# Four tiles of the first expert taken from six attention blocks and multiplied beside the routing, with the next weights split at other places

## The chip, the cores and the metric

One core of one Trainium2 chip runs the whole program. The metric is the device time of one execution in microseconds (us). In the profile PE is TensorE (matmuls) and PEld its weight loads, DVE is VectorE, ACT is ScalarE, POOL is GpSimd and SP is SyncE, which only starts transfers. A line number such as L853 is a line of the kernel before.

## What is computed

Three layers follow each other: an attention over pooled keys, a mixture of experts in which each token goes to one expert, and a mixture in which each token goes through all experts.

```python
# B, H, S, D = 4, 8, 576, 64; pool = 8
k_p = k.reshape(B, H, Sp, pool, D).mean(axis=3)
v_p = v.reshape(B, H, Sp, pool, D).mean(axis=3)
attn = softmax(scale * np.matmul(q, k_p.transpose(0, 1, 3, 2)))
x = (attn @ v_p).transpose(0, 2, 1, 3).reshape(B * S, H * D)
...
# first mixture: N, D, E, F = 2304, 512, 8, 1024
logits = x @ w_gate
e_idx = np.argmax(logits, axis=1)
for e in range(E):
    mask = e_idx == e
    h = np.maximum(x[mask] @ w1[e], 0.0)
    out[mask] = gate_w[mask, None] * eom[mask, e, None] * (h @ w2[e])
...
# second mixture: P from 8 alternating normalisations of exp(logits)
for e in range(E):
    h = np.maximum(x @ w1[e], 0.0)
    out += P[:, e:e + 1] * (h @ w2[e])
```

With the inputs that are used, expert 0 gets 1217 of the 2304 tokens, which is ten tiles of 128 positions; four other experts have 5, 2, 3 and 2 tiles.

## The kernel before, in words

**The planned part.** The attention, the routing of the first mixture and the first expert's first tile are not emitted as they are written. `Notes`, a subclass of `Plan`, records each operation with what it reads and writes, with a cost and with a number; `Plan.run` is a list scheduler that gives each engine, whenever it is free in the model, the ready operation with the lowest number plus `late`. A larger `late` puts an operation behind others, and `after` makes all operations recorded from then on wait for one earlier operation. What comes out is a fixed order for each engine. All these instructions carry the line of the recorder, L1293. Accumulation groups of matmuls stay together unless `whole` is false. The four PSUM tiles of this part are called ab.

**The attention** works on nine blocks of 256 rows in the order 0, 1, 2, 3, 4, 5, 8, 6, 7. `weigh` multiplies the probabilities with the values and divides; `write_rows` writes the block's rows of x to `rowd` in DRAM; `top1` turns the gate logits of a range of the 18 token tiles into one-hot rows `oh` (called at blocks 3, 8, 6 and 7). `between` loads the first expert's weights in eight pieces into the six raw buffers `wr` and splits each into a high and a low 16-bit part, which later stand in `w1` and `w2` (slots wa and wb).

**The routing.** `route` ranks all tokens by expert: it counts the one-hot rows with matmuls (`ones`, `prior`, `tri`), makes a one-hot row per token tile on VectorE, and by 18 more matmuls gets `idx`, the list of tokens in order of expert. 18 indirect transfers (`gather`, on POOL's queue) bring 128 rows each from `rowd` into one of eight buffers `raw` (`GB` = 8). `columns` transposes a gathered tile with four matmuls against the identity and splits it into high and low parts of `xT` (ScalarE copies the high part, VectorE subtracts). `stages` and `registers` put the tile counts and the starts of the experts into registers.

**A tile of an expert** is `one`: 96 matmuls of 128x128 for the first product (three 16-bit products for each of 4 x 8 blocks, L853), the ReLU on ScalarE (L858), the cast to 16 bit and the subtraction that gives the low part, both on VectorE (L859, L860), 24 matmuls of 128x512 for the second product (L868), the scaling and adding into `x2` (L873) and the row maximum (L876), on VectorE.

**The first expert.** Ten sets of columns and tile 0 stand in the planned part. Then `moe1` runs a loop over c = 1 to 8, each under a branch on the tile count, with four more sets of columns behind c = 1 and c = 2 and one piece of the next expert's weights behind each (`w[1].step(c - 1)`: a scaled copy on ScalarE and a subtraction on VectorE, L785). Tile 9 follows under its own branch.

**Then** `ahead` gives POOL the preparation of the second mixture's first weights (L976 to L1013: loads, sums, casts and stores, all on POOL), and nested branches (`stage`, `item`) go through the other experts. In the first two tiles of an expert the eight pieces of the next expert's weights are split: `pieces` says which stand ahead of the first product, between its two halves and behind both.

Of the kernel before, what the change touches and what calls it, by code (L numbers as in the profile page):

```python
# [10 lines left out]
F32 = mybir.dt.float32  # L11
# [372 lines left out]
LATE = {"scores": -50, "weigh": 150, "key_layout": 100}  # L384


def attention(g):
# [12 lines left out]
    def load(b, i):  # L400
        kv[b, i] = put(load_kv, b, i)
# [4 lines left out]

    load(0, 0)
# [17 lines left out]
    for at, n in enumerate(order):  # L425
        qT = g.tile([P, 2, H, P], F16, "qT", 2)
        put(q_transpose, qb[n], qT)
        if at + 3 < NB:
            qb[order[at + 3]] = put(q_load, order[at + 3])
        ex = g.tile([P, 2, H, SP], F32, "ex", 2)  # L430
        for hf in range(2):
            put(scores, n, qT, ex, hf)
        eT = g.tile([P, 2, 2, CH, P], F16, "eT", 2)
        for tail in (False, True):
            put(exp_transpose, ex, eT, tail)
        xs = g.tile([P, 2, H, VC - 1], F32, "xs", 3)
# [233 lines left out]
def stages(g):  # L670
# [46 lines left out]
    nc.vector.tensor_copy(g.stgi, stg[:, 0:3])  # L717
# [12 lines left out]
def registers(g):  # L730
# [6 lines left out]
        min_val=0, max_val=NT,  # L737
    )
# [8 lines left out]
class Weights:  # L747
# [19 lines left out]
    def raw(self, i):  # L767
        return self.g.wr[(8 * self.stage + i) % RAW]
# [26 lines left out]
GB = 8  # L795


def gather(g, j):

    gr = g.gat[:, j % GB]  # L800
    g.nc.gpsimd.indirect_dma_start(
        out=gr,
        out_offset=None,
        in_=g.rowd,
        in_offset=bass.IndirectOffsetOnAxis(ap=g.idx[:, j:j + 1], axis=0),
        bounds_check=N - 1,
        oob_is_err=False,
    )
    g.rows[j] = gr


def gathered(g, first, last):
    for j in range(first, last):
        columns(g, j, g.rows.pop(j))
        if j + GB < NT:
            gather(g, j + GB)


def columns(g, j, gr):
# [8 lines left out]
    hi, lo = [g.xT[:, s, :, j * P:(j + 1) * P] for s in range(2)]  # L828
# [4 lines left out]
def one(g, w, xt, j, cm, middle=None):  # L833
# [14 lines left out]
    for m, ph in enumerate(phs):  # L848
# [10 lines left out]
        nc.vector.tensor_copy(hs[:, 0, sl], hr[:, sl])  # L859
# [21 lines left out]
def moe1(g, first):  # L881
# [9 lines left out]
    xts = []  # L891
    for i in range(4):
        xt = g.xt.tile([P, 2, KC, P], F16, name=f"xt{i}")
        xts.append(xt)
# [9 lines left out]
    def item(r, c, xt):  # L904
# [1226 lines left out]
def attention_moe_moe(ctx: ExitStack, tc, q, k, v, wg, wo, w1, w2, wgb, w1b, w2b, out):  # L2131
# [50 lines left out]
    g.stgi = g.per.tile([P, 3, E], I32, name="stgi")  # L2182
# [31 lines left out]
    first = Weights(g, 0, w1[0], w2[0])  # L2214

# [14 lines left out]
    with ExitStack() as c:  # L2230
# [3 lines left out]
        attention(g)  # L2234
        g.tile = Arena(wb).tile
        route(g)
        g.notes.late = 300
        for i in range(6):
            g.nc.scalar.activation(
                g.x2[:, i * 3:i * 3 + 3, :].rearrange("p t c -> p (t c)"),  # L2240
                g.zero.to_broadcast([P, 3 * DM]), AF.Copy,
            )
# [81 lines left out]
```

## Time and profile before

| what | value |
|---|---|
| median of 3 runs | 1787.71 us (1787.49 to 1789.68) |
| the profiled execution | 1778.33 us, its span 1776.6 us |
| PE busy | 1693.8 us (95%) |
| PEld busy | 1475.0 us (83%) |
| DVE busy | 1267.4 us (71%) |
| ACT busy | 1023.1 us (58%) |
| POOL busy | 280.8 us (16%) |

Times in the trace count from the start of the span. The attention's last matmul ends at 117.42, the loop over the first expert's tiles begins at 153.23 and its tile 9 at 242.28, the second expert begins at 256.65 and the second mixture's work near 411. In a row of the timeline the first number is the start, the second the duration of the group, "x24" the number of instructions in it, and the bracket the idle time of the engine ahead of it with what ended it. In the table by stretch each engine's busy time stands with its number of instructions; PEclk is TensorE's granted clock as a share of the full 2.4 GHz.

### The profile page before, as it was taken

The page shows a single profiled execution, that of the slowest core. Times are in us where ns is not written, and L with a number is a line of the kernel's source. Part 1 is how long each engine was busy: PE and PEld are TensorE (multiplying, and loading weights), DVE is VectorE, ACT ScalarE, POOL GpSimd, SP SyncE. Part 2 cuts the span into 40 slices and gives each one's busy share as a digit, 9 for nine tenths or more (in the row PEclk, how much of TensorE's full clock was granted, in tenths as well). Part 3 has the DMA queues.
Part 4 walks back from the last instruction along what each step waited for, and adds up shares of the span by engine and source line. Part 5 has one row for each costly group of instructions (what it writes and reads, how often), then busy time and mean ns, then how long its engine had stood idle before and what let it go on. Part 6 is the DMA issues. An engine that isn't in the chain of part 4 may idle for free. (4 is left out here: it accounts for less than half of the span.)

```text
span 1776.6 us, 40042 instructions
## 1 busy us (share of the span) xinstructions
PE 1693.8 (95%) x17079; PEld 1475.0 (83%) x17079; DVE 1267.4 (71%) x2262; ACT 1023.1 (58%) x1872; POOL 280.8 (16%) x300
## 2 busy tenths in 40 slices
PE   5769998897999999999999999999999999999997
PEld 4657765666998899889888988898899889888986
DVE  7885567667896885787588567856876786587664
ACT  4743221435577775776577557756765775576542
POOL 7833778200000000000000000000000000000011
PEclk9989999998999999999999999999999999999999
DMA  9625434447331242243133313422441242234211
GB/s 301 164 72 179 138 120 160 136 158 301 103 134 56 88 141 37 48 109 107 27 82 114 78 25 81 137 47 37 114 125 25 60 133 71 37 72 125 102 54 42
DMA packets 83167, 183.83 MB, mean 103 GB/s; under 512 B 27664, under 2 KB 35856, under 8 KB 81168
## 3 DMA queue, kind: packets, MB, share of 16 engines
q1 hardware_dynamic: 68912, 131.66, 22.3%
q0 software_dynamic: 14048, 49.29, 13.0%
q8 instruction: 145, 2.38, 0.5%
q14 instruction: 62, 0.51, 0.1%
HBM read 121.16 MB, written 59.77 MB: 102 GB/s over the span
## 5 line engine op out<-in xcount | busy, mean ns | idle before, releaser
L1797 PEld LDWEIGHTS <-w1c 128*128 128x128 f16 x6720 | 604.0, 98 | 64.2 <-issue 2.2
L1896 PEld LDWEIGHTS <-hs 128*128 128x128 f16 x6048 | 590.6, 98 | 69.8 <-issue 1.9
L1797 PE MATMUL ua<-xc,w1c 128*128 128x256 f16 (+1 forms) x3840 | 426.7, 262 | 0.8 <-DVE xc L1460 0.6
L1896 PE MATMUL da<-x,hs 128*128 128x256 f16 x2592 | 318.2, 273 | 1.4 <-ACT z L1434 0.9
L1959 POOL DMA_DIRECT2D sums<-x x54 | 45.9, 850 | 1252.0 <-ACT x L1436 1217.0
L1797 PE MATMUL uc<-xc,w1c 128*128 128x256 f16 (+1 forms) x1920 | 213.1, 262 | 0.7 <-DVE xc L1460 0.5
L1817 DVE TENSOR_TENSOR u<-u,uc 128x512 f32<-128x512 f32 x144 | 99.0, 687 | 75.9 <-ACT u L1434 61.0
L1817 DVE TENSOR_TENSOR p<-p,ub 128x512 f32<-128x512 f32 x72 | 49.5, 687 | 140.8 <-PE ub L1797 140.8
L1434 ACT COPY u<-ua 128x512 f32<-128x512 f32 x144 | 83.9, 583 | 86.8 <-PE ua L1797 85.3
L1460 DVE TENSOR_TENSOR hs<-h,hs 128x512 f16<-128x512 f32 x144 | 99.2, 689 | 43.2 <-ACT hs L1434 43.2
L1460 DVE TENSOR_TENSOR hs<-u,hs 128x512 f16<-128x512 f32 x144 | 99.2, 689 | 39.2 <-ACT hs L1434 39.2
L1436 ACT ACTIVATE u<-u 128x512 f32<-128x512 f32 x144 | 91.0, 632 | 38.6 <-DVE u L1817 38.6
L858 ACT ACTIVATE wa<-ph 128x512 f32<-128x512 f32 x42 | 25.1, 597 | 150.7 <-PE ph L853 78.7
L1797 PE MATMUL ub<-xc,w1c 128*128 128x256 f16 (+1 forms) x960 | 106.3, 262 | 0.0
L1896 PE MATMUL da<-w2r,hs 128*128 128x256 f16 x864 | 106.1, 273 | 0.0
L1896 PE MATMUL db<-x,hs 128*128 128x256 f16 x864 | 106.1, 273 | 0.0
L1896 PE MATMUL dc<-x,hs 128*128 128x256 f16 x864 | 106.1, 273 | 0.0
L1896 PE MATMUL dc<-w2r,hs 128*128 128x256 f16 x864 | 106.1, 273 | 0.0
L868 PEld LDWEIGHTS <-wa 128*128 128x128 f16 x504 | 46.8, 98 | 70.4 <-DVE wa L860 13.0
L1434 ACT CAST hs<-p 128x512 f16<-128x512 f32 x144 | 89.3, 620 | 26.4 <-DVE p L1460 26.1
L1460 DVE TENSOR_TENSOR hs<-p,hs 128x512 f16<-128x512 f32 x144 | 99.0, 687 | 0.6 <-ACT hs L1434 0.6
L1436 ACT ACTIVATE p<-p 128x512 f32<-128x512 f32 x72 | 45.2, 628 | 86.2 <-DVE p L1817 86.2
(271 smaller groups left out, 2592.3 us busy)
## 6 DMA issues: line engine op xcount, KB each, us to landing
raw<-in_moe_w_dram SPq DMA_DIRECT2D x56, 512.0 KB, 4.0
wr<-in_moe_w_dram SPq DMA_DIRECT2D x54, 512.0 KB, 4.2
sums<-x POOLq DMA_DIRECT2D x54, 512.0 KB, 5.1
xc<-cspill SPq DMA_DIRECT2D x14, 1792.0 KB, 7.3
cspill<-xc SPq DMA_DIRECT2D x8, 896.0 KB, 4.5
sums<-x SPq DMA_DIRECT2D x9, 512.0 KB, 3.4
x<-sums SPq DMA_DIRECT2D x9, 512.0 KB, 3.6
wa<-in_k_dram SPq DMA_DIRECT2D x4, 1024.0 KB, 10.7
```

Source lines behind the costliest of these rows:

```text
L858: nc.scalar.activation(hr[:, sl], ph, AF.Relu, scale=HSC)
L868: nc.tensor.matmul(py, hs[:, a, k, :], w.w2[:, b, k, :], start=(k == 0 and t == 0), stop=(k == FC - 1 and t == 2),)
L1434: self.nc.scalar.copy(o, x)
L1436: self.nc.scalar.activation(o, x, func, scale=scale)
L1460: lambda: e.tensor_tensor(o, x, y, op=op), reads, writes, late,
L1797: nc.tensor.matmul(o, g.w1c[:, l, a, k, f * P:(f + 1) * P], g.xc[:, pr, r, b, k, :], start=(first and fi == 0 and n == 0), stop=(n == 5), ...
L1817: lambda: nc_.tensor_tensor(o_[0], o_[0], x_[0], op=ALU.add),
L1896: nc.tensor.matmul(t[x][0][:, lo], g.hs[:, sl[f // 2], l, a, f % 2, :], g.w2c[r][:, b, f, :], start=(first and n == 0), stop=(n == 11), sk ...
L1959: lambda: nc.gpsimd.dma_start(sums, x, accum_op=ALU.add), xk, [sk],
```

## The change

- `early_rows` ranks the tokens of blocks 0 to 5 (twelve token tiles) that belong to expert 0, for the first four tiles of 128: a count, a rank, twelve one-hot rows with twelve matmuls, and an index of four columns. `top1` is called after block 5 for tiles 8 to 11 in addition. Four indirect transfers bring the rows into two of the raw weight buffers (wr2 and wr3), and four calls of `columns` make xt0 to xt3 of them.
- `early_tiles` multiplies these four tiles in the planned part, with `late` 300 and not ahead of the last block's transposes of probabilities. ScalarE keeps the unscaled results in the gather buffers; `early_out` scales them after the routing.
- `full` says which of the four early tiles had 128 tokens. A tile that had fewer is multiplied again in a branch behind the loop; five registers (`s_a`) carry this.
- The routing's gathers go in the order 4, 5, ..., 17, 0, ..., 3. The planned part ends with tile 4, and the loop runs over c = 5 to 8 with two weight pieces behind each.
- The other experts' weight pieces move: none ahead of the first product, one (piece 0 or 5) between the halves, four or two behind both. The cast to 16 bit in `one` goes from VectorE to ScalarE. The raw buffers of later stages are shifted by two.
- Two transfers write zeros to rows of `rowd` that a gather of tiles 0 to 11 can touch before they are written; `x2` is cleared in seven pieces, for tiles 4 to 17.

**VectorE at the end of the attention.** x holds a block's results, ab the PSUM tiles, wa the row sums. Before:

```order
L1293 SCALAR_TENSOR_TENSOR x_97<-ab_277,x_97 128x2x512
L1293 TENSOR_REDUCE lgt<-x_97 128x32
L1293 SCALAR_TENSOR_TENSOR x_97<-ab_275,x_97 64x2x128
L1293 TENSOR_REDUCE mx<-lgt 128x6
L1293 TENSOR_TENSOR eq<-lgt,mx 128x48
L1293 TENSOR_TENSOR eq<-eq,rev 128x48
L1293 TENSOR_REDUCE fi<-eq 128x6
L1293 TENSOR_SCALAR wa<-ab_276 128x8
```

After, with the last early one-hot rows (out of iof), the early index (xT out of ab_296) and the early columns xt:

```order
L1446 TENSOR_SCALAR x_97<-iof_117,xT 128x128 x2
L1446 SCALAR_TENSOR_TENSOR x_97<-ab_294,x_97 128x2x512
L1446 TENSOR_SCALAR xT<-ab_296 128x4
L1446 TENSOR_SCALAR wa<-ab_295 128x8
L1446 TENSOR_TENSOR xT<-xT,ab_296 128x4
L1446 RECIPROCAL wa<-wa 128x8
L1446 TENSOR_TENSOR x_97<-ab_295,wa 128x640
L1446 SCALAR_TENSOR_TENSOR x_97<-ab_293,x_97 64x2x128
L1446 TENSOR_TENSOR xt_171<-ab_293,xt_171 128x512
```

The index is complete at its fifth row, the first subtraction of a gathered tile is the ninth, and the last blocks' divisions and logits stand behind it.

**TensorE behind the attention's last matmul.** oh holds the one-hot rows of all tokens, wa the first expert's weights. Before:

```order
L1293 MATMUL ab_274<-xT,x_97 128x81
L1293 LDWEIGHTS oh
L1293 MATMUL ab_277<-ones_115,oh 128x128
L1293 MATMUL ab_277<-ones_115,oh 16x128
L1293 LDWEIGHTS wb
L1293 MATMUL ab_275<-prior,wb 128x144
```

After:

```order
L1446 MATMUL ab_296<-xT,x_97 128x81
L1446 LDWEIGHTS wa
L1446 MATMUL ab_294<-xt_171,wa 128x128
L1446 LDWEIGHTS oh
L1446 MATMUL ab_293<-ones_115,oh 128x128
L1446 MATMUL ab_293<-ones_115,oh 16x128
L1446 MATMUL ab_295<-wa 128x512
L1446 LDWEIGHTS wb
L1446 MATMUL ab_296<-prior,wb 128x144
```

84 matmuls of the first early tile stand ahead of the routing's first, and its other 12 and one of its second product ahead of the ranking with prior. The early tiles' other matmuls stand between the later steps of the routing.

```diff
@@ attention
-        if n in (3, 8, 6, 7):
-            put(top1, *{3: (0, 8), 8: (16, 18), 6: (8, 14), 7: (14, 16)}[n])
+        if n in (3, 5, 8, 6, 7):
+            put(top1, *{3: (0, 8), 5: (8, 12), 8: (16, 18), 6: (12, 14), 7: (14, 16)}[n])
+        if n == 5:
+            put(early_rows)
@@ Weights
     def raw(self, i):
-        return self.g.wr[(8 * self.stage + i) % RAW]
+        return self.g.wr[(8 * self.stage + 2 * (self.stage > 0) + i) % RAW]
@@
+NE = 4
+EB = 6
+ORDER = [*range(NE, NT), *range(NE)]
...
+def early_rows(g):
...
+    for t in range(T):
+        ohp = new([P, P], BF16, "eohp", 3)
+        nc.vector.tensor_scalar(
+            ohp, g.iof16, lof[:, 0, t:t + 1], 1.0, op0=ALU.is_equal, op1=ALU.mult
+        )
+        nc.tensor.matmul(
+            px[:, 0, 0:2 * NE], ohp, ohv[:, t].rearrange("p x j -> p (x j)"),
+            start=(t == 0), stop=(t == T - 1),
+        )
...
+    for c in range(NE):
+        gather_rows(g, g.early[c], idx[:, c:c + 1], EB // 2 * S - 64)
+    for c in range(NE):
+        columns(g, g.early[c], g.xts[c])
+
+
+def early_tiles(g, w):
+
+    for c in range(NE):
+        product(g, w, g.xts[c], lambda py, c=c: g.nc.scalar.copy(g.early[c], py), c)
...
+def early_out(g):
...
+    nc.vector.tensor_tensor(ce, g.cm[:, 0, 0:NE], g.full, op=ALU.mult)
+    for c in range(NE):
+        nc.vector.tensor_scalar(g.x2[:, c], g.early[c], ce[:, c:c + 1], None, op0=ALU.mult)
...
+def product(g, w, xt, out, half):
+
+    nc = g.nc
+    hr, hs = g.hid[0]
...
@@ one
-        nc.vector.tensor_copy(hs[:, 0, sl], hr[:, sl])
+        nc.scalar.copy(hs[:, 0, sl], hr[:, sl])
@@ moe1
-            pieces = (((0,), (1, 2), (3, 4)), ((5,), (6,), (7,)))[c]
+            pieces = (((), (0,), (1, 2, 3, 4)), ((), (5,), (6, 7)))[c]
...
-    for c in range(1, 9):
+    for c in range(NE + 1, 9):
         first_tiles(c)
-        if c < 3:
-            gathered(g, NT - GB * (3 - c) // 2, NT - GB * (2 - c) // 2)
-        w[1].step(c - 1)
+        i = c - NE - 1
+        if i < 2:
+            gathered(g, NT - GB * (2 - i) // 2, NT - GB * (1 - i) // 2)
+        w[1].step(2 * i, 2 * i + 1)
+    with tc.If(g.s_a[NE] > 0):
+        for c in range(NE):
+            with tc.If(g.s_a[c] > 0):
+                one(
...
@@ the planned part
         attention(g)
+        g.notes.late, g.notes.after = 300, g.spread
+        early_tiles(g, first)
+        g.notes.late, g.notes.after = 0, None
...
+        early_out(g)
         gathered(g, 0, NT - GB)
-        one(g, first, g.xT[:, :, :, 0:P], slice(0, 1), g.cm[:, 0, 0:1])
+        one(
+            g, first, g.xT[:, :, :, NE * P:(NE + 1) * P], slice(NE, NE + 1),
+            g.cm[:, 0, NE:NE + 1],
+        )
```

## Rows read from the trace of the kernel before

**Rows 1.** The busy time of each engine by stretch, for two stretches.

```profile
core 0: us, PE busy (x) PEld busy (x) DVE busy (x) ACT busy (x) POOL busy (x), PEclk, DMA share, GB/s
80.00:116.00 36.00, 31.09 (x624) 26.92 (x624) 34.49 (x77) 20.23 (x25) 13.55 (x8) 0.97 0.33 75
117.40:153.20 35.80, 22.21 (x204) 16.36 (x203) 26.87 (x113) 11.61 (x17) 22.40 (x22) 0.76 0.48 152
```

**Rows 2.** TensorE's timeline from the attention's last matmul to the loop's last tile.

```profile
113.03 4.39 PE L1293 MATMUL ab<-xT,x 128*128 128x81 f16 x70 [1.02 <-DVE x L1293]
120.42 0.38 PE L1293 MATMUL ab<-ones,oh 128*128 128x128 bf16 x2 [3.00 <-DVE oh L1293]
...
126.27 2.09 PE L1293 MATMUL ab<-wb 128*128 128x36 bf16 x18 [3.97 <-POOL wb L1293]
...
136.29 2.35 PE L1293 MATMUL ab<-xT,wa 128*128 128x128 f16 x24
...
153.23 5.52 PE L853 MATMUL ph<-xT,wa 128*128 128x128 f16 x96 [0.94 <-DVE x L1293]
158.59 5.34 PE L868 MATMUL py<-wa 128*128 128x512 f16 x24
163.77 1.91 PE L827 MATMUL py<-ident,raw 128*128 128x128 f32 x16
165.52 5.52 PE L853 MATMUL ph<-xT,wa 128*128 128x128 f16 x96
...
242.28 5.52 PE L853 MATMUL ph<-xT,wa 128*128 128x128 f16 x96
```

**Rows 3.** Timelines of VectorE, POOL and TensorE, from the index to the first gathered tile.

```profile
128.61 0.17 DVE L1293 TENSOR_TENSOR idx<-wb,ab 128x18 int32<-128x18 f32 x1
129.08 1.27 POOL L1293 DMA_INDIRECT raw<-rowd,idx  x1 [1.72 <-DVE wb L1293]
130.66 1.00 POOL L1293 DMA_INDIRECT raw<-rowd,idx  x1 [0.31 <-issue]
132.72 1.12 PE L1293 MATMUL ab<-ident,raw 128*128 128x128 f32 x4 [4.36 <-DMA raw<-rowd,idx]
134.54 0.69 DVE L1293 TENSOR_TENSOR xT<-ab,xT 128x512 f16<-128x512 f32 x1 [2.91 <-ACT xT L1293]
```

**Rows 4.** VectorE's timeline: a wait near the attention's end, and the routing's one-hot rows.

```profile
117.45 0.17 DVE L1293 TENSOR_SCALAR wa<-ab 128x8 f32<-128x8 f32 x1 [1.43 <-PE ab L1293]
...
124.23 3.86 DVE L1293 TENSOR_SCALAR wb<-iof,wb 128x128 bf16<-128x128 bf16 x16
```

**Rows 5.** Timelines of TensorE and VectorE: experts two and three, weight splits L785.

```profile
256.65 7.15 PE L853 MATMUL ph<-xt,wb 128*128 128x128 f16 x96 [2.86 <-DVE xt L897]
270.48 3.78 DVE L785 SCALAR_TENSOR_TENSOR wa<-wr,wa 128x1024 f16<-128x1024 f32 x2
274.33 5.66 PE L853 MATMUL ph<-xt,wb 128*128 128x128 f16 x96
288.31 5.52 PE L853 MATMUL ph<-xt,wb 128*128 128x128 f16 x96
328.77 2.35 DVE L785 SCALAR_TENSOR_TENSOR wb<-wr,wb 128x1024 f16<-128x1024 f32 x2
334.42 5.52 PE L853 MATMUL ph<-xt,wa 128*128 128x128 f16 x96
```

**Rows 6.** TensorE's timeline at the starts of experts three and five.

```profile
323.38 5.52 PE L853 MATMUL ph<-xt,wa 128*128 128x128 f16 x96 [2.02 <-PEq L925]
...
380.41 5.52 PE L853 MATMUL ph<-xt,wa 128*128 128x128 f16 x96 [1.15 <-PEq L925]
391.98 5.52 PE L853 MATMUL ph<-xt,wa 128*128 128x128 f16 x96
```

**Rows 7.** POOL's timeline: first load and last store of the second mixture's weights.

```profile
178.27 0.58 POOL L976 DMA_DIRECT2D raw<-in_moe_w_dram  x1 [24.59 <-PE py L827]
...
323.81 0.68 POOL L1006 DMA_DIRECT2D w2spill<-raw  x1 [0.30 <-POOL raw L1002]
```

More of the change, by code (lines that the diff above doesn't have):

```diff
@@ L405, in sums @@
         vp[b] = put(pool_sum, nc.gpsimd if b else nc.vector, kv[b, 1])
+    none = g.tile([64, DM], F32, "none")
+    nc.gpsimd.memset(none, 0.0)
+    for b in range(EB // 2 - 1):
+        nc.sync.dma_start(g.rowd[b * S + 512:(b + 1) * S, :], none)
     load(0, 0)
@@ L435, in attention @@
             put(exp_transpose, ex, eT, tail)
+        g.spread = len(g.notes.tasks) - 1
         xs = g.tile([P, 2, H, VC - 1], F32, "xs", 3)
@@ L737, in registers @@
         min_val=0, max_val=NT,
+    )
+    _, g.s_a = nc.values_load_multi_w_load_instructions(
+        tab[:, 3 * E:3 * E + NE + 1], engines=[ET.PE, ET.DVE, ET.Activation, ET.SP],
+        min_val=0, max_val=NE,
     )
@@ L795, with gather_rows @@
 GB = 8
-def gather(g, j):
-    gr = g.gat[:, j % GB]
+NE = 4
+EB = 6
+ORDER = [*range(NE, NT), *range(NE)]
+def gather_rows(g, gr, idx, n=N):
     g.nc.gpsimd.indirect_dma_start(
@@ L803, in gather @@
         out_offset=None,
-        in_=g.rowd,
-        in_offset=bass.IndirectOffsetOnAxis(ap=g.idx[:, j:j + 1], axis=0),
-        bounds_check=N - 1,
+        in_=g.rowd[0:n, :],
+        in_offset=bass.IndirectOffsetOnAxis(ap=idx, axis=0),
+        bounds_check=n - 1,
         oob_is_err=False,
     )
+def gather(g, i):
+    gr = g.gat[:, i % GB]
+    j = ORDER[i]
+    gather_rows(g, gr, g.idx[:, j:j + 1])
     g.rows[j] = gr
 def gathered(g, first, last):
[L813 to L816, printed above, removed]
@@ new lines, in product @@
+def product(g, w, xt, out, half):
+    nc = g.nc
+    hr, hs = g.hid[0]
+    any2 = bank2(g)
+    for m in range(2):
+        ph = any2[:, m].rearrange("p (f n) -> p f n", n=P)
+        for mm in range(4):
+            f = 4 * m + mm
+            for k in range(KC):
+                for t, (a, b) in enumerate(PASSES):
+                    nc.tensor.matmul(
+                        ph[:, mm, :], w.w1[:, a, k, f * P:(f + 1) * P], xt[:, b, k, :],
+                        start=(k == 0 and t == 0), stop=(k == KC - 1 and t == 2),
+                    )
+        sl = slice(4 * m, 4 * m + 4)
+        nc.scalar.activation(hr[:, sl], ph, AF.Relu, scale=HSC)
+        nc.scalar.copy(hs[:, 0, sl], hr[:, sl])
+        nc.vector.tensor_tensor(hs[:, 1, sl], hr[:, sl], hs[:, 0, sl], op=ALU.subtract)
+    py = bank2(g)[:, 0]
+    g.notes.whole = False
+    for k in range(FC):
+        for t, (a, b) in enumerate(PASSES):
+            nc.tensor.matmul(
+                py, hs[:, a, k, :], w.w2[:, b, k, :],
+                start=(k == 0 and t == 0), stop=(k == FC - 1 and t == 2),
+            )
+    g.notes.whole = True
+    out(py)
@@ L820, in columns @@
+def columns(g, gr, xt):
     nc = g.nc
@@ L827, in columns @@
         nc.tensor.transpose(pt[:, k, :], gr[:, k * P:(k + 1) * P], g.ident)
-    hi, lo = [g.xT[:, s, :, j * P:(j + 1) * P] for s in range(2)]
+    hi, lo = [xt[:, s] for s in range(2)]
     nc.scalar.copy(hi, pt)
@@ L890, in moe1 @@
     ]
[L891 to L894, printed above, removed]
+    xts = g.xts
     def fetch(c, j):
@@ L2181, in attention_moe_moe @@
     g.cm = g.per.tile([P, E, NT], F32, name="cm")
-    g.stgi = g.per.tile([P, 3, E], I32, name="stgi")
+    g.stgi = g.per.tile([P, 4, E], I32, name="stgi")
     g.idx = g.keep.tile([P, NT], I32, name="idx")
@@ L2214, in attention_moe_moe @@
     first = Weights(g, 0, w1[0], w2[0])
+    g.early = [g.wr[2 + i // 2][:, i % 2 * DM:(i % 2 + 1) * DM] for i in range(NE)]
+    g.xts = []
+    for i in range(4):
+        t = g.xt.tile([P, 2, KC, P], F16, name=f"xt{i}")
+        g.xts.append(t)
+    g.full = g.per.tile([P, NE], F32, name="full")
     def between(n):
@@ L2237, in attention_moe_moe @@
         g.notes.late = 300
-        for i in range(6):
+        for i in range(NE, NT, 2):
             g.nc.scalar.activation(
-                g.x2[:, i * 3:i * 3 + 3, :].rearrange("p t c -> p (t c)"),
-                g.zero.to_broadcast([P, 3 * DM]), AF.Copy,
+                g.x2[:, i:i + 2, :].rearrange("p t c -> p (t c)"),
+                g.zero.to_broadcast([P, 2 * DM]), AF.Copy,
             )
```

75 lines of the change are left out of this document (72 added, 3 removed).

## The prediction

> **What bounds the kernel now.** I read the busy time by stretch first, then VectorE's rows and waits in the attention, then the chain from the token list to the first gathered tile, then TensorE's rows up to the second layer. The chain that ended last holds only the final output writes, so the bound of each stretch is read from the engines. The reader should see three things.
>
> First, late in the attention VectorE is full: 34.49 us of the 36 between 80 and 116 us [rows 1]. Work added there before the last block's logits moves the end of the attention by its own length.
>
> Second, from the last attention matmul (113.03 + 4.39 = 117.42) to the first tile of the expert loop (153.23) TensorE works 22.2 of 35.8 us at a mean granted clock of 0.76 [rows 1, 2]. It waits 3.00 for the last one-hot and 4.36 for the first gathered rows, and what follows that wait runs slowly: 24 matmuls in 2.35 us, 98 ns each, against 5.36 / 96 = 56 ns in the loop [rows 2, 3]. This is the room that the change wants to fill.
>
> Third, in the loop TensorE hardly waits. A tile is 5.36 for the first product (153.23 to 158.59) and 5.18 for the second (to 163.77): 10.54 us, and 1.75 more if four tiles are transposed behind it [rows 2]. The eight tiles of the loop take 89.05 (153.23 to 242.28). The second layer starts behind the last expert, so what moves that point moves the end.
>
> The profiled execution took 1778.33 (span 1776.6), 9.4 less than the median of the runs, 1787.71. The sum below is a difference and is put on the median.
>
> **The change part by part.**
>
> *a. The early ranking, inside the attention: +11, from +6 to +15.* Before the last one-hot VectorE gets 35 more instructions: twelve one-hot rows of 128x128 at 3.86 / 16 = 0.24 [rows 4], 2.9; four subtractions of 128x512 at 0.69 [rows 3], 2.7; 19 small ones at up to 0.17 each, as the index's own [rows 3], 3.2 at most. Between other instructions small ones overlap, so I take 8.0 for 8.8. With VectorE full, all of it shows.
>
> Then comes a wait that the attention did not have. From the index's write (128.78) to the first transpose of gathered rows (132.72) the kernel takes 3.94, and VectorE's subtraction starts at 134.54, 5.8 after the index [rows 3]; at full clock 0.5 less, 5.2. In the new order only three VectorE instructions (1.3 us) lie between the early index and the first early subtraction, so VectorE stands still for 3.9. TensorE stands before the first early transposes too, with 63 matmuls of block 8 behind it that the next VectorE instruction needs; that adds 1.4. Back come the 1.43 wait near the end [rows 4], where TensorE will be ahead, and 0.5 of smaller waits. 8.0 + 5.3 - 1.9 = 11.4, rounded to 11. Low end: no gather wait. High end: TensorE falls to its 1.2 GHz level behind that wait, as the matmuls at 136.29 ran, and the 63 matmuls take twice their 4.0 (4.39 / 70 each [rows 2]).
>
> The four early gathers cost POOL 1.3 each (1.00 + 0.31) [rows 3], 5.2 us where it has nothing else: taken as nothing. The two transfers of zeros (0.26 MB) stand in SP's queue behind six weight loads and ahead of the next keys: nothing, at worst 0.26 MB at the 75 GB/s of the late attention [rows 1], 3.5. Block 8's row writes now wait on SP for the early gathers; the writes of blocks 6 and 7 queue behind them, but are made later anyway.
>
> *b. From the last attention matmul to the loop: 35.8 becomes 67.5, +31.7.* TensorE has to do five tiles at 10.54 (52.7), ten sets of transposes at 1.91 / 4 = 0.48 [rows 2] (4.8) and the routing's own matmuls (2.9, an estimate from its first and its largest group, 0.38 and 2.09 [rows 2], some of it at full clock): 60.4 us, all at full clock since it hardly pauses. By the new order it still waits: after the last routing matmul 36 matmuls (2.0) stand ahead of the first gathered rows that are 4 us off, so 2.0; gathers come every 1.3 us and four sets of transposes (0.48 each) follow each other without filler, 2.1; the hidden tile's one buffer is handed over twice at the end, 1.5; 0.6 elsewhere. 6.2 in all, and 0.9 to enter the loop, as now [rows 2]. ScalarE and VectorE get six short steps per tile, of 0.7 or less, beside it. The routing itself starts 0.5 to 1 later because the first early product stands ahead of its first matmul; that lies inside the 60.4.
>
> *c. The loop: -42.9.* Eight tiles become four. The two with transposes stay (12.29 each, 153.23 to 165.52 [rows 2]); the other six take 64.5, 10.75 each, and two of them stay: 89.05 - 24.6 - 21.5 = 42.9. Each now carries two weight splits, 2.35 us of VectorE [rows 5] in 10.5.
>
> *d. The skipped repeat: +1.5.* The block that would multiply early tiles again is jumped over by all engines. Its nearest rows are the jumps at the end of an expert: 1.15 and 2.02 of TensorE [rows 6]; all of it shows, since TensorE has nothing queued. Bounds: 0.9, the present entry of the loop [rows 2], and 2.9, the longest wait at an expert's start [rows 5]. The five more registers are read in that entry: nothing.
>
> *e. The other experts: -4, from -8 to +6.* Expert two's first two tiles take 17.68 and 13.98 (256.65 to 288.31) instead of 10.54: 10.6 lost, because eight weight splits stand between VectorE's own steps of the tile, at 1.89 each while POOL prepares the second layer's weights, against 1.18 when POOL is done (3.78 and 2.35 a pair) [rows 5]. Expert three's first takes 11.04, with POOL's work over [rows 5 to 7]. Now one split stands between the halves and four behind both, and the cast to 16 bit leaves VectorE for ScalarE. With POOL idle I count no stall. With POOL busy the four splits (7.6) and the tile's other steps outlast the 10.5 of TensorE and the next tile waits some 3. But POOL's work, 145 us long (178.27 to 323.81) [rows 7], starts 25 us into the loop, so 42 us later than now, and then lies beside experts three and four as well. Three contended experts at 3, with 1.6 of slow clock once (7.15 against 5.52 [rows 5]), are 10.6. Today's losses are 10.6 in expert two, 0.5 in three and 1.0 each in the split tiles of four and five (391.98 - 380.41 = 11.57 [rows 6]), 13.1; the cast gives 1 more: -3.5, rounded to -4.
>
> The row shows a split slowed by 60% beside POOL. The Trainium skill (SBUF — State Buffer, section "SBUF: two separate sides") says more: VectorE with two SBUF inputs and GpSimd share a port that one of them holds for its whole instruction while the other is blocked. By that rule every split behind a POOL step would lose up to the whole step, experts three and four would pay about what expert two paid, and the sum would end above zero; by the row it stays below. The rows agree with a loss, not with a full block each time.
>
> **Sum:** 11 + 31.7 - 42.9 + 1.5 - 4 = -2.7, so 1785.0. The 42 us taken out of the loop are nearly all put back ahead of it, because the room there held only 35.8 - 22.2 = 13.6 idle us and some 6 of slow clock, and the ranking costs 11.
>
> **The rivals.**
>
> *The early work finds room (1777).* If VectorE's queue has been ordered so that the early gathers land while it is still busy, a is 6 instead of 11, and with gathers ahead of TensorE b loses 3 of its 6.2: -2.7 - 5 - 3 = -10.7. For it: POOL and SP are idle there. Against it: VectorE's 34.49 of 36, and three instructions between index and subtraction.
>
> *POOL's work meets the later splits (1795).* Slower: the splits of experts three and four run beside POOL's preparation. Stage e becomes +6 if each pays some 5 us, half of what expert two paid: -2.7 + 10 = +7.3. It decides from the point where their splits take over 1.6 us instead of 1.18. For it: the 42 us shift. Against it: the cast is gone from VectorE and the four splits stand behind both halves.
>
> *The change does not do what it says (1827).* If the first expert had fewer than 512 tokens in blocks 0 to 5, tiles would be multiplied again, up to 42.2 more: -2.7 + 42.2 = +39.5. Evaluating the reference's routing on its own inputs gives 571, and a first expert of ten tiles, which the loop's nine plus one show; hardly possible.
>
> **How the numbers follow.** 0.2% is 3.6 us, about what a measurement tells from no change. Forecast 0.50, its own range 1780 to 1791; room found 0.20; POOL's work 0.28; repeat 0.02. The forecast lies below -3.6 in about 0.42 of its cases and above +3.6 in 0.05, the second case wholly below, the third nearly wholly above: faster 0.41, same 0.26, slower 0.33. The range 1774 to 1799 takes in both middle cases with the bounds of a and e, and leaves out the repeat.
>
> **What would show it.** The loop's first tile at 194 to 198 instead of 153.23. A wait of 3 to 5 us of VectorE for a subtraction of an early tile near 113. TensorE at clock 1.0 between the attention and the loop, with under 8 us idle. POOL's last spill near 365. No split pair over 3.2 us beside a TensorE wait over 3 in experts three and four. The forecast is wrong if the loop starts before 190 or after 200, or if experts two to five together gain or lose over 8 us.

## The result, and the profile after

The change made the kernel slower: 1800.71 us (1798.64 to 1804.31, four runs) against 1787.6 of the kernel before on the same chip, a ratio of 1.0075 [1.0056, 1.0094]. That is 13.1 us more, against a forecast of 2.7 less, and 1.7 above the upper end of the range. The profiled execution took 1804.31 us. Its page begins:

```profile
span 1802.5 us, 40215 instructions
## 1 busy us (share of the span) xinstructions
PE 1710.8 (95%) x17110; PEld 1490.0 (83%) x17110; DVE 1262.7 (70%) x2261; ACT 1052.3 (58%) x1926; POOL 294.3 (16%) x305
```

TensorE's busy time grew by 17.0 us (1693.8 before) although the products of the experts are the same ones. The busy time by stretch says where, with the columns of [rows 1]. The stretches are: start to the last one-hot, from there to the loop, the loop, the rest of the experts, the way to the second mixture, and late attention once more:

```profile
0.00:138.70 138.70, 102.58 (x1349) 87.73 (x1350) 110.55 (x271) 71.07 (x93) 84.28 (x95) 0.89 0.60 174
138.70:211.80 73.10, 63.53 (x635) 45.11 (x633) 34.02 (x126) 21.93 (x38) 22.41 (x22) 0.93 0.36 115
211.80:260.80 49.00, 46.22 (x513) 34.07 (x514) 27.40 (x32) 21.43 (x32) 19.04 (x20) 1.00 0.32 109
260.80:423.00 162.20, 145.57 (x1560) 103.13 (x1560) 109.87 (x101) 62.09 (x84) 104.10 (x97) 0.96 0.49 165
423.00:436.80 13.80, 0.03 (x2) 0.06 (x1) 2.96 (x10) 0.00 (x0) 0.00 (x0) 0.68 0.39 123
80.00:116.00 36.00, 29.70 (x428) 26.18 (x429) 28.72 (x75) 14.48 (x19) 13.04 (x9) 0.77 0.14 31
```

The last row answers to the first of [rows 1]. Before, VectorE was full there (34.49 of 36) and TensorE ran at 0.97; now VectorE is busy for 28.72 and TensorE's mean granted clock is 0.77. The attention has not only more to do, it stalls. TensorE's timeline after, which answers to [rows 2, 5, 6]:

```profile
135.77 3.52 PE L1446 MATMUL ab<-xt,wa 128*128 128x128 f16 x60
...
154.64 0.82 PE L1446 MATMUL ab<-ident,raw 128*128 128x128 f32 x4 [2.13 <-DMA raw<-rowd,idx]
157.17 1.44 PE L1446 MATMUL ab<-xt,wa 128*128 128x128 f16 x12 [1.71 <-issue]
...
211.79 3.40 PE L1001 MATMUL ph<-xT,wa 128*128 128x128 f16 x58 [0.94 <-DVE x L1446]
...
260.77 1.73 PE L1001 MATMUL ph<-xT,wa 128*128 128x128 f16 x28 [1.49 <-PEq L1096]
...
293.92 6.61 PE L1016 MATMUL py<-wb,wa 128*128 128x512 f16 x22 [3.30 <-DVE wa L1008]
...
436.78 3.44 PE L1742 MATMUL pt<-ident,x 128*128 128x128 f32 x14 [13.77 <-DVE x L1735]
```

The early products stand where the routing was (135.77), and the wait for the first gathered rows is down from 4.36 to 2.13: the room is filled, as meant. The loop begins at 211.79, tile 9 at 260.77 (before: 242.28), and the second mixture waits 13.77 for its first transposes.

VectorE late in the attention, answering to [rows 3, 4]; then POOL, with the first early gather and the first load of the second mixture's weights [rows 7]:

```profile
116.79 0.15 DVE L1446 TENSOR_TENSOR xT<-xT,ab 128x4 int32<-128x4 f32 x1
117.89 0.41 DVE L1446 SCALAR_TENSOR_TENSOR x<-ab,x 64x256 f16<-64x256 f32 x1
122.94 0.69 DVE L1446 TENSOR_TENSOR xt<-ab,xt 128x512 f16<-128x512 f32 x1 [4.65 <-ACT xt L1446]
125.57 0.17 DVE L1446 TENSOR_SCALAR wa<-ab 128x8 f32<-128x8 f32 x1 [1.94 <-PE ab L1446]
138.69 0.18 DVE L1446 TENSOR_TENSOR oh<-fi,rev 128x16 bf16<-128x16 f32 x1
```

```profile
117.23 1.27 POOL L1446 DMA_INDIRECT wr<-rowd,xT  x1 [17.24 <-DVE wa L1446]
...
236.87 0.59 POOL L1129 DMA_DIRECT2D raw<-in_moe_w_dram  x1 [59.46 <-PE py L975]
```

The index (116.79) is followed by the forecast wait of VectorE for the first early subtraction, 4.65, and a second of 1.94. The last one-hot is at 138.69. POOL begins the second mixture's weights 58.6 us later than before (178.27).

### The profile page after: what moved, and what is told of

The parts are those of the page before. It is cut to its first block, busy times and chain, and to the rows that moved or that the text cites. A ratio compares the mean times of both kernels' runs of the same rounds, so it can differ in the third digit from the quotient of the medians.

```text
span 1802.5 us, 40215 instructions
## 1 busy us (share of the span) xinstructions
PE 1710.8 (95%) x17110; PEld 1490.0 (83%) x17110; DVE 1262.7 (70%) x2261; ACT 1052.3 (58%) x1926; POOL 294.3 (16%) x305
## 5 line engine op out<-in xcount | busy, mean ns | idle before, releaser
L1970 DVE TENSOR_TENSOR u<-u,uc 128x512 f32<-128x512 f32 x144 | 98.7, 686 | 76.5 <-ACT u L1587 61.7
L1587 ACT CAST hs<-h 128x512 f16<-128x512 f32 x144 | 89.3, 620 | 4.3 <-DVE h L1613 2.9
L1587 ACT CAST hs<-u 128x512 f16<-128x512 f32 x144 | 89.0, 618 | 3.1 <-DVE u L1613 1.3
```

The costliest lines, as they stand in the source:

```text
L1587: self.nc.scalar.copy(o, x)
L1970: lambda: nc_.tensor_tensor(o_[0], o_[0], x_[0], op=ALU.add),
```

## The experiments

All ratios are to the kernel before on the same chip. From the traces come four marks: the last one-hot, the loop's first tile, tile 9, and the end of the experts' last product.

**Both kernels once more**, to have a pair of traces from one chip.

> The kernel before once more, for a second trace and its spread. The trace before (span 1776.6) lies 9 us under the median of its runs (1787.6), the trace after (1802.5) 3 over its own. If the before trace was simply a quick execution, this one has a span near 1786, and the extra time shows in one stretch: either between the last attention matmul (117.4) and the second layer's first matmul (411.8), or behind it, where both traces took 1365 us. If the comparison stretch by stretch holds, the loop's first tile starts within 1 us of 153.2 and the second layer within 2 of 411.8. Time: the same, 0.999 to 1.001.

> The changed kernel once more. In its first trace TensorE's results were seen late by ScalarE three times behind the routing's first gathers (the ReLU starts 4.2 us after its matmuls, the first two casts of gathered tiles 4 us after their transposes), and TensorE ran at 0.64 of its clock from 154.6 to 164.0. If this belongs to the program, it is here again with the loop's first tile at 209 to 214. If it was chance of that one execution, the loop starts near 201. Time: 1.006 to 1.009 of before.

Before again: 1.0003 [0.999, 1.0016], its profiled execution 1788.17. After again: 1.0080 [1.0062, 1.0098], 1798.29. This changed the reading. The trace that the prediction was made from is of an execution 9.4 us below the median, and the second one of the same program loses that much in one place: from the last one-hot to the loop it takes 42.7 us, not 33. Its rows of TensorE, ScalarE and VectorE there:

```profile
139.93 0.28 PE L1293 MATMUL ab<-ident,raw 128*128 128x128 f32 x1
140.68 0.27 PE L1293 MATMUL ab<-ident,raw 128*128 128x128 f32 x1 [0.48 <-issue]
...
143.59 0.38 PE L1293 MATMUL ab<-xT,wa 128*128 128x128 f16 x4 [1.02 <-issue]
...
145.09 1.07 ACT L1293 CAST xT<-ab 128x512 f16<-128x512 f32 x2 [7.68 <-remote]
...
145.71 0.69 DVE L1293 TENSOR_TENSOR xT<-ab,xT 128x512 f16<-128x512 f32 x1 [7.00 <-issue]
```

While the indirect gathers run, TensorE's transposes come one at a time with gaps of half a microsecond in which the trace shows no wait, and ScalarE sees their results late. The kernel after has the same (a wait of 1.71 for "issue" at 157.17 above). From here on the balance is made against this second trace; per stage, the mean of the two traces of after less this one:

| stage | forecast | measured |
|---|---|---|
| a, start to last one-hot | +11 | +18.4 |
| b, last one-hot to loop | +31.7 | +30.5 |
| c and d, loop and repeat, to tile 9 | -41.4 | -40.7 |
| e, tile 9 to the last product | -4 | +1.7 |
| last product to the second mixture | 0 | +3.4 |
| the rest | 0 | -0.3 |
| sum | -2.7 | +13.1 |

The last one-hot alone varies between traces: five kernels with the attention of before have it at 119.78 to 123.24, a spread of 3.5 us with a mean of 121.1, and five with the attention of after at 135.79 to 138.69. A difference of two or three us between single traces is therefore no finding.

**The ranking alone.** Before plus the added call and `early_rows`, whose index is not used:

```diff
-        if n in (3, 8, 6, 7):
+        if n in (3, 5, 8, 6, 7):
...
+        if n == 5:
+            put(early_rows)
```

> The kernel before with the early ranking alone: block 5's one-hot rows are made in time, tokens are counted and ranked and the early index is made, but nothing is gathered, transposed or multiplied early (the result is the reference's). The attention of the change ends 18.4 us later than that of before; VectorE is busy 8.3 us more in it and idle 9.8 us more. Theory 1, VectorE's own work for the ranking shows in full: 29 added instructions of 6.5 us and 4 us in which small ones wait for GpSimd's splits; the last one-hot comes 6 to 9 us later than 120.2, and the time is 1794 to 1797. Theory 2, the gathers and what waits for them make nearly all of it: the last one-hot comes 2 to 4 us later and the time is 1790 to 1792.

Measured: 1.0022 [1.0012, 1.0033], +4.1 us; the last one-hot at 127.60, 6.5 above the mean of 121.1 and 4.4 above the one trace of that attention from the same chip (123.24). The mark fits theory 1, the time theory 2; the ranking costs 4 to 6.5.

**The ranking and the gathered columns, without their products.** The zero transfers, the four gathers and `columns` stay; the tiles they make are not used.

```diff
+    for c in range(NE):
+        gather_rows(g, g.early[c], idx[:, c:c + 1], EB // 2 * S - 64)
+    for c in range(NE):
+        early_columns(g, g.early[c], g.xts[c])
```

> The early ranking, and with it the two transfers of zeros, the four early gathers, their transposes, casts and subtractions; the gathered tiles are then not used, and everything behind is as in the kernel before (the result is the reference's). The ranking alone cost 4.1 us. Theory 1, the wait for the gathers in the middle of the attention is what step a sized too small: 7 to 11 us on top, +11 to +15 over before, last one-hot 11 to 15 us later. Theory 2, the attention of the change is long because of the multiplications that are fed into it: at most 5 us on top, +6 to +9.

Measured: 1.0087 [1.0073, 1.0102], +15.8, a little over theory 1; the last one-hot at 139.42, as in the whole change. The loss of stage a needs no early product: the ranking makes a quarter to a third of it, what belongs to the gathered columns the rest.

**The gather's wait.** The same with four plain transfers in the gathers' place, of rows that have been in DRAM for long, so that nothing waits for the index; the columns are still ordered behind the index, and are not used. Beside it the kernel above once more.

```diff
-        gather_rows(g, g.early[c], idx[:, c:c + 1], EB // 2 * S - 64)
+        nc.sync.dma_start(g.early[c], g.rowd[c * P:(c + 1) * P, :])
```

> As gather_only, but the four early buffers are loaded with the first 512 rows of the attention's result by plain transfers that do not need the early index; the ranking, the transposes, casts and subtractions stay where they are in every engine's order up to the first subtraction, the following ones stand right behind it (the gathered tiles are not used, the result is the reference's). Theory 1, the wait between the early index and the first subtraction (4.4 us and 1.3 behind it in gather_only) is the price that step a sized too small: the attention ends 5 to 7 us earlier than gather_only's. Theory 2, VectorE's small instructions that stand behind GpSimd's splits, and TensorE's fall to half clock after them, make up the rest: these stay (three of 1.4 to 1.8 us instead of 0.2; a granted clock of 0.5 to 0.6 between 100 and 110), and the last one-hot still comes 9 us later than in the kernel before.

> gather_only again, on the same chip as plain_rows: last one-hot at 138 to 140, 13 to 17 us slower than before.

Measured: 1.0082 [1.0062, 1.0102], +14.5, with the last one-hot at 134.81; and 1.0108 [1.0084, 1.0132], +21.1, with the last one-hot at 144.35. The repetition missed its expectation on both counts; its trace is of the slowest of its four executions, 1811.05. Without the gathers it is 6.6 faster on the same chip, and still 14.5 slower than before. VectorE's first early subtractions, with the gathers and then without:

```profile
123.82 0.69 DVE L1388 TENSOR_TENSOR xt<-ab,xt 128x512 f16<-128x512 f32 x1 [4.41 <-ACT xt L1388]
```

```profile
120.61 0.69 DVE L1391 TENSOR_TENSOR xt<-ab,xt 128x512 f16<-128x512 f32 x1
121.64 1.89 DVE L1391 TENSOR_TENSOR xt<-ab,xt 128x512 f16<-128x512 f32 x3 [0.34 <-ACT xt L1391]
```

The wait of 4.41 is gone. From block 5's one-hot rows to the last ones it is 30.2 us instead of 36.0 and 36.9, and 27.05 with the ranking alone. So the gathers cost 5.8 to 6.7 there, and the columns' own work is 3.1. But block 5's one-hot rows come later in the ten traces with early columns (101.4 to 104.6, once 107.4, against 100.55 with the ranking alone), before any token is ranked. Their row maximum (`mx`) does not: it stands at 94.9 to 98.1, once 100.9, mean 96.6, against 96.54. So the two early transfers of zeros, which the kernel with the ranking alone does not have, and the order up to there cost nothing that shows. From the maximum to the one-hot rows it is 6.5 in each of the ten, against 4.0. Small VectorE instructions of `top1` at block 5, after once more, with POOL beside them, and then the ranking alone:

```profile
94.41 6.32 POOL L1446 TENSOR_TENSOR wa<-wr,wa 128x1024 f16<-128x1024 f32 x3
...
97.26 1.43 DVE L1446 TENSOR_TENSOR eq<-lgt,mx 128x32 f32<-128x32 f32 x1
98.61 0.74 DVE L1446 TENSOR_TENSOR x<-ab,wa 128x576 f32<-128x576 f32 x1
99.28 1.50 DVE L1446 TENSOR_TENSOR eq<-eq,rev 128x32 f32<-128x32 f32 x1
```

```profile
97.30 0.19 DVE L1357 TENSOR_TENSOR eq<-lgt,mx 128x32 f32<-128x32 f32 x1
98.09 0.18 DVE L1357 TENSOR_TENSOR eq<-eq,rev 128x32 f32<-128x32 f32 x1
```

POOL's group is three weight splits of some 2.1 each, which end near 96.5, 98.6 and 100.7. The two comparisons, which read two operands in SBUF, end at 98.7 and 100.8, each with a step of POOL; the multiplication between them, which reads `ab` in PSUM, takes its usual 0.74. With the ranking alone POOL's group had ended at 96.7, ahead of both comparisons. The ten traces all have these two (1.42 to 1.43 and 1.49 to 1.50), 2.5 us more than the 0.37 that they take without POOL beside them. At block 3 after once more has two more (1.25 and 1.76, from 75.00 to 78.3) where before again has one (1.52 at 80.83); behind the two TensorE waits 3.58 for VectorE's x, and then its clock falls. The busy time from 80 to 90 and from 100 to 110 us, before again and after again:

```profile
80.00:90.00 10.00, 7.69 (x193) 6.75 (x194) 9.57 (x22) 6.73 (x8) 7.28 (x5) 1.00 0.24 55
100.00:110.00 10.00, 9.80 (x191) 8.48 (x190) 9.47 (x20) 5.49 (x7) 0.00 (x0) 1.00 0.14 30
```

```profile
80.00:90.00 10.00, 9.36 (x107) 8.48 (x108) 5.82 (x22) 4.07 (x6) 4.40 (x5) 0.69 0.01 2
100.00:110.00 10.00, 6.57 (x48) 5.95 (x49) 8.09 (x21) 2.30 (x5) 0.72 (x1) 0.50 0.00 0
```

From 100 to 110 TensorE is at its 1.2 GHz level throughout; it had waited 1.08 for VectorE just before and waits 2.27 more there. So the two comparisons beside POOL are the 2.5 us that are lost before the early work. What the fall of the clock adds behind them is not separated: no run took either away alone.

**Another place for the early columns.** The four calls of `columns` behind the last block's transposes of probabilities.

```diff
-    for c in range(NE):
-        columns(g, g.early[c], g.xts[c])
...
+        for c in range(NE):
+            columns(g, g.early[c], g.xts[c])
```

> The transposes and subtractions of the four early gathered tiles stand behind the last block's transposes of probabilities; 26 VectorE instructions instead of 3 lie between the early index and the first early subtraction. Theory 1, the wait for the early gathers in VectorE's order (4.65 and 1.94 us in the trace after) is on the attention's path: the attention ends 5 to 8 us earlier and the kernel takes 5 to 8 us less than the change, 1793 to 1796. Theory 2, the lost time is VectorE's own added work and the wait only takes the place of others: less than 2 us.

Measured: 1.0061 [1.0046, 1.0076], 3.0 below after on the same chip, which is hardly clear of the noise; the last one-hot at 136.36, within the 135.79 to 138.69 of the old place. By the times the place is worth some 3 us, not the 5 to 8 of theory 1. The reason is not that the wait for the rows has moved: no early column is due where VectorE now stands still. TensorE, ScalarE and VectorE beside the four early gathers, which POOL issues from 116.35 to 121.54:

```profile
120.76 0.36 PE L1444 MATMUL ab<-xT,x 128*128 128x81 f16 x5 [0.38 <-issue]
...
122.29 1.28 ACT L1444 ACTIVATE x<-ab 128x1024 f16<-128x1024 f32 x2 [6.33 <-remote]
...
122.38 0.17 DVE L1444 TENSOR_SCALAR wa<-ab 128x8 f32<-128x8 f32 x1 [5.55 <-remote]
```

From 119 on TensorE's matmuls of the attention come five or six at a time with gaps of 0.38, and ScalarE and VectorE go on only after the last gather has been issued. It looks like the slow stretch of before again, now inside the attention; the kernel with three remedies below, which has the columns at this place too, shows it as well (6.38 and 5.59). At the old place TensorE waits 1.3 to 2.7 for the rows themselves. Plain transfers take away both, so the 5.8 to 6.7 are the price of the gathers, not of the place alone.

**The old places of the weight splits**, with the cast back on VectorE.

```diff
-        nc.scalar.copy(hs[:, 0, sl], hr[:, sl])
+        nc.vector.tensor_copy(hs[:, 0, sl], hr[:, sl])
...
-            pieces = (((), (0,), (1, 2, 3, 4)), ((), (5,), (6, 7)))[c]
+            pieces = (((0,), (1, 2), (3, 4)), ((5,), (6,), (7,)))[c]
```

> Only the other experts are as before: the old places of the weight pieces and the cast to 16 bit on VectorE (the early tiles stay). The prediction's step e said the new places give 4 us: then this takes 4 us more than the change, and experts two to five 153 us instead of 149. The rival: with POOL's preparation 58 us later beside experts three and four, the new places are worth nothing or cost: this takes the same or up to 3 us less.

Measured: 1.0099 [1.0083, 1.0116], 3.6 above after; tile 9 to the last product 167.7 instead of 161. The new places help. **The same part by itself**, put into the kernel before, and then the cast alone:

> The kernel before with the new places of the weight pieces and the cast on ScalarE alone. Against the old places the change gained 4 us by them (1801.2 against 1805.2). If they help by the splits that stand between VectorE's steps, expert two's first two tiles lose less than their 10.6 us here too: 1781 to 1785, faster than before. The rival: without the late preparation on GpSimd the old places were good enough for experts three to five, and the way out of the branches costs 3 us more with the new ones: 1787 to 1789.

> The kernel before with only the cast to 16 bit moved from VectorE to ScalarE; the pieces stay at their old places. New places and cast together gave 7.6 us. Theory 1, the cast matters, because it takes two of VectorE's steps out of each tile in which weights are split: 4 to 7 us faster than before. Theory 2, the places matter (splits behind both halves): 0 to 2 us.

Measured: 0.9949 [0.9936, 0.9962], 7.6 us faster, and 0.9963 [0.995, 0.9975], 7.4 faster. Most of the gain is the cast (by the means of the runs 8.1 and 6.5).

**POOL earlier.** All sets of columns in the planned part, none in the loop, so that POOL's gathers are over before the loop and its preparation starts sooner.

```diff
-        gathered(g, 0, NT - GB)
+        gathered(g, 0, NT)
...
-        if i < 2:
-            gathered(g, NT - GB * (2 - i) // 2, NT - GB * (1 - i) // 2)
```

> The change with all 14 column sets of gathered tiles in the planned part, none in the loop, so that the gather buffers come free some 24 us earlier and GpSimd's preparation of the second mixture's weights starts near 212 instead of 237. The work on TensorE is the same. Theory 1, the weight splits of experts three to five lose time beside that preparation because it starts late: it now ends near 357 instead of 380, and the time is 3 to 6 us under the change, 1795 to 1798. Theory 2, the experts lose by the order of splits in the tile alone: the same time as the change.

Measured: 1.0031 [1.0018, 1.0044], +5.7 where after has 13.1 to 13.4. POOL's first load, at 236.87 in after, moves forward by 51 us:

```profile
185.94 0.59 POOL L1127 DMA_DIRECT2D raw<-in_moe_w_dram  x1 [12.08 <-PE ab L1444]
```

Tile 9 to the last product takes 150.7 instead of 161. Four kernels with the new places and an early POOL have 149.4, 144.1, 150.7 and 154.6 (the last is the kernel with three remedies below); four with the new places and a late POOL 162.2, 160.3, 158.9 and 160.5. Before again, with the old places and an early POOL, has 159.6.

**Without the repeat.** The branch that multiplies early tiles again is left out, and its registers; with this routing it is never entered.

> The change without the branch that multiplies early tiles again, and without its five registers; with these inputs the branch is never taken. The prediction's step d gave it 1.5 us: tile 9 starts 1 to 2 us earlier behind tile 8 and the time is 1799 to 1800. The rival: the four engines fetch new code behind the skipped block, which the change pays once more at the end of the experts: 3 to 5 us, 1796 to 1798.

Measured: 1.0055 [1.004, 1.0069], 10.1 above before where after has 13.1. The difference of 3 is between two chips and not clear of the noise. The traces show the branch at tile 9: TensorE waits 0.33 to 1.49 behind it, and then once more inside the first product, without a named wait,

```profile
263.57 3.96 PE L1001 MATMUL ph<-xT,wa 128*128 128x128 f16 x68 [1.07 <-issue]
```

together 1.4 to 2.7 in five traces with the branch, and neither in the two without. Between the forecast of step d and the rival of 3 to 5 us this does not decide.

**Two combinations.** The early work with its three remedies (columns elsewhere, sets planned, no repeat), and on the other side the kernel before with the new places, the cast and all sets planned:

> The change with three repairs at once: the early transposes behind the last block's (cols_spread, 2.5 us less than the change), all column sets in the planned part (7 us less), no branch for a repeat (3 us less). Theory 1, these add up: +13 - 12.5, within 2 us of the kernel before. Even so it is 6 to 9 us behind before with the new tail, which has no early tiles: then early multiplication itself loses. Theory 2, with them repaired the early tiles pay: faster than before with the new tail (more than 8 us faster than before).

> The kernel before with the new places and the cast, and all column sets in the planned part, so that GpSimd's preparation starts some 12 us earlier (near 170 instead of 183). If its overlap with the experts' splits is what costs there, 2 to 4 us are gained on the 7.6: 10 to 12 us faster than before. The rival: expert two's splits lie beside the preparation either way, and the sets fill no room ahead of the loop: 6 to 8 us faster.

Measured: 1.0020 [1.0011, 1.0029], 2.8 slower than before; and 0.9942 [0.9924, 0.9961], 13.1 faster by the medians, 10.8 by the means. The second beats both kernels and has no early tile in it; that the planned sets add to the 7.6 of the new places and the cast is not clear of the noise. On this chip the early work with its remedies costs 14 to 16 us. This is nearer to theory 1: the remedies bring the early work close to before, and it still loses. The groups of instructions of the other experts (busy time, mean ns of one, idle time before), for the splits beside POOL: before again,

```profile
L785 DVE SCALAR_TENSOR_TENSOR wa<-wr,wa 128x1024 f16<-128x1024 f32 x16 | 26.6, 1684 | 0.4 <-ACT wa L784 0.4
```

after again,

```profile
L813 DVE SCALAR_TENSOR_TENSOR wa<-wr,wa 128x1024 f16<-128x1024 f32 x16 | 32.2, 2054 | 0.3 <-ACT wa L812 0.3
```

and the last kernel:

```profile
L785 DVE SCALAR_TENSOR_TENSOR wa<-wr,wa 128x1024 f16<-128x1024 f32 x16 | 22.3, 1434 | 1.4 <-ACT wa L784 1.3
```

TensorE's waits for VectorE's halves of the hidden tile in the same stretch (us in total, times, longest): before again, where VectorE also makes the cast,

```profile
PE py L868 <- DVE wa L859: 6.5, 6, 3.2
...
PE py L868 <- DVE wa L860: 1.9, 3, 1.0
```

after again,

```profile
PE py L1016 <- DVE wa L1008: 9.5, 6, 3.3
```

and the last kernel:

```profile
PE py L868 <- DVE wa L860: 0.4, 1, 0.4
```

One split takes 1684, 2054 and 1434 ns, and the waits come to 8.4, 9.5 and 0.4 us: slower splits, longer waits. The kernel with all sets planned, which differs from after in nothing but the place of the sets, lies between with 1628 ns and 4.7 us.

## Why the prediction was wrong

The forecast missed by 15.8 us: 7.4 of them in a, 5.7 in e and 3.4 in a step that it did not have; b came 1.2 better than forecast, c and d together 0.7 worse.

**The step that failed by sign is e, "-4".** It held that with four splits behind both halves and the cast gone the loss beside POOL would stay at 3 us a contended expert, less than today. Measured: +1.7. Two parts of it were right. The new places and the cast gain (before with them is 7.6 faster; taking them from after costs 3.6), and POOL's work does move beside experts three and four. The price was wrong: with the new places the late POOL costs some 10 us (161 against 150.7 with the sets planned; 6 against the slowest of the four kernels with an early POOL), with the old ones 8 (167.7 against 159.6): more than the 7.6 that the places and the cast give, or about as much. This is the mechanism of the rival "POOL's work meets the later splits". Its condition, splits over 1.6 us, is met by one of the two groups of after again (2054 ns; the other has 1511), and stage e came out at +1.7, between the forecast's -4 and the rival's +6. The forecast moved POOL's start by 42 us; it was 49 against before again, as much later as the loop began.

**The step that failed by size is a, "11.4, rounded to 11".** Its two positive terms came out near their size, the first partly by luck. VectorE's busy time up to the last one-hot is 8.3 us longer, forecast 8.0, but 2.5 of the 8.3 are the two comparisons of block 5 that stood beside POOL; before again and after again:

```profile
0.00:120.30 120.30, 89.26 (x1265) 76.27 (x1265) 101.56 (x235) 70.78 (x89) 78.90 (x90) 0.95 0.69 190
```

```profile
0.00:138.40 138.40, 103.41 (x1351) 88.52 (x1352) 109.83 (x271) 71.02 (x93) 84.11 (x95) 0.90 0.59 175
```

The gathers cost 5.8 to 6.7, forecast 5.3. What failed is "Back come the 1.43 wait near the end [rows 4], where TensorE will be ahead, and 0.5 of smaller waits": VectorE's idle time grew by 9.8 (28.57 less 18.74 in these rows), not by 3.4. Nothing came back, and 2.5 us were lost before the early work, at block 5. By the single runs stage a is 6.5 for the ranking, 3.1 for the columns, 5.8 for the gathers and 2.5 for the comparisons, 17.9 of 18.4. The assumption behind the sum, "With VectorE full, all of it shows", left out that VectorE is idle for 18.74 of the 120 us, and that added work moves who stands beside whom. With other instructions in the scheduler's list the order of the blocks before changed too, comparisons fell beside POOL's splits, and TensorE waited and dropped to its lower clock. The bound that had this, "TensorE falls to its 1.2 GHz level", was put behind the gather and priced at 4; the fall came earlier.

The comparisons at blocks 3 and 5 end together with POOL's steps, and the multiplication from PSUM between them does not wait. The prediction had weighed a rule of the Trainium skill (SBUF — State Buffer, section "SBUF: two separate sides"), that VectorE with two SBUF inputs and a GpSimd step that reads SBUF block each other for a whole instruction, and had gone by the milder row; these rows agree with the full block. A sum above zero, which the rule gave by way of the later experts, is what was measured, but only 5.7 us of the miss lie there.

**A step that was missing** is the way out of the experts' branches. From the last product to the second mixture's first matmul, before needs 9.2 (9.8 again), the kernel before with the new places 10.2 to 11.0, the kernels with early tiles and the new places 12.1 to 13.8: +3.4 on average. The early tiles with the old places and the cast on VectorE have 9.9. So, by this one trace, the loss comes with the new places and the cast, and takes back half of the 6.4 that they gain between tile 9 and the last product (167.7 against 161.3). Why it is larger with early tiles than without them stays open.

**Right were b and c.** From the last one-hot to the loop +30.5 measured, +31.7 forecast; loop and repeat together -40.7, forecast -41.4. TensorE is busy 63.5 of 73.1 us where 60.4 of 67.5 were forecast. Both the 67.5 and the 35.8 that it was set against lack the slow stretch beside the gathers, which the trace of the prediction happened not to show; it falls into both kernels, and the difference stands. Where the stretch is not slow (the chip of the ranking alone), the kernel without the repeat takes 66.7 from the last one-hot to the loop, and the two with nothing early to multiply 33.2 and 34.7: a difference of 32 to 33.5. The granted clock is 0.93 there, not 1.0, and over 8 us are idle (9.57). **d** was forecast at 1.5, with bounds of 0.9 and 2.9; the traces show 1.4 to 2.7.

Of what was to be seen, the loop's first tile at 194 to 198 came at 211.79, over the 200 named as the point from which the forecast is wrong. Of the 15.9 that it missed 195.9 by (153.23 + 11 + 31.7), 7.5 are a's, and 8.4 lie in the stretch beside the gathers. POOL's last spill, expected near 365, came at 392.41. In experts three and four a row of four splits took 8.19, a pair 4.1, but TensorE's longest wait for VectorE was 2.57. Experts two to five changed by less than the 8 us that were named.

## What to carry to other kernels

Work put into a stretch that is idle on one engine still has to be fetched and prepared by others. Here four tiles saved 41 us in the loop, took 31 of them back in the gap, and paid 18 for the ranking and gathering that had to go into a full stretch. Moving an engine's background work is part of the price: ask beside what it will run then, and try the small parts of a change by themselves, because the cast, the new places and the planned sets alone gave 11 to 13 us, and the large part took more than that.

## What the runs showed of the hardware

- While 128-row indirect gathers were in flight, TensorE's transposes came singly, with gaps of 0.45 to 0.48, and ScalarE's and VectorE's next steps on their results 4.20 (after) to 7.68 us (before again) late, with no wait named that explains it. Beside four such gathers in the attention (another place for the early columns) it was gaps of 0.38, 6.33 and 5.55. The long stretch is in most traces, small in the first one and on a chip where the kernel before takes 1780.23; its cause is open.
- The kernel before has medians of 1780.23, 1785.64, 1788.24 and 1788.82 us on different chips, a spread of 0.5%, larger than several effects measured here. Only ratios on one chip were used.
- A comparison of 128x32 on VectorE that takes 0.18 us alone took 1.43 and 1.50 beside POOL's splits of 2.1, ending with them, in all ten traces with early columns; a multiplication of 128x576 with one operand in PSUM, between the two, took its usual 0.74.
